# Chunked attention and a gated feed-forward: a planner's choice of engine, order and margin for copies and attention operations

## The chip, the cores and the metric

The kernel runs on one core of a Trainium2 chip. The metric is the device time of one execution in microseconds, the median of several executions. Its engines are called PE (TensorE, matrix products), PEld (TensorE's weight loads), DVE (VectorE), ACT (ScalarE), POOL (GpSimd) and SP (SyncE) in the profile; each works through its own queue in order, and semaphores hold an instruction back until what it needs is done. An instruction that waits holds up all that stand behind it on its engine.

## The reference

Chunked attention with a small memory, and then a gated feed-forward network on its output. Batch 4, 8 heads, 768 positions, 64 numbers a head; 8 memory slots; 3072 tokens, model width 512, inner width 1536; all float32.

```python
for c in range(nc):                          # 24 chunks of 32 positions
    l_start, r_end = max(0, 32*c - 16), min(S, 32*c + 32 + 8)
    k_full = concatenate([mem_k, k[:, :, l_start:r_end]], axis=2)
    v_full = concatenate([mem_v, v[:, :, l_start:r_end]], axis=2)
    scores = scale * matmul(q_c, k_full.transpose(0, 1, 3, 2))
    a = softmax(scores)
    out[:, :, c_start:c_end] = matmul(a, v_full)
x = out.transpose(0, 2, 1, 3).reshape(B * S, H * D)
y = (maximum(x @ w_gate, 0) * (x @ w_val)) @ w_out
```

So each chunk of 32 queries sees 16 positions before it, its own 32, 8 after it and 8 memory slots: 64 slots in all.

## The kernel before, in words

**Tiles.** The 3072 tokens are 24 tiles of 128 (4 chunks each), six tiles a batch. For the feed-forward part they are joined into eight blocks of 2, 2, 2, 4, 4, 4, 4 and 2 tiles (`BLOCKS`), so that block 2 is tiles 4 and 5, block 3 is tiles 6 to 9 and block 4 is tiles 10 to 13.

**Attention of a tile** `a`, each step an operation with a name:
- `t`, `tc`: keys and queries are transposed, by TensorE against an identity (`qk_t`, L275; for batch 0 `pair_t`, L236) into a PSUM slot of the pool `aps`, and copied out by VectorE or ScalarE (`qk_copy`, L79 or L81 of the helper `copy`). From tile 15 on a DMA transposes instead.
- `s`: scores, 32 small products (L309) into the one slot of the pool `sps`.
- `max`, `sub`: VectorE takes the row maximum (L322) and subtracts it (L329); that frees the slot of the scores.
- `exp`: ScalarE, three instructions (L337). `sum`, `rec`, `nrm`: VectorE (L341, L345, L352).
- `p`, `pc`: the probabilities are transposed on TensorE (L358) and copied out; from tile 15 by a DMA.
- `v`, `x`: products with the values (L388; for batch 0 L374 and L381) into a slot of `aps`, copied out into the block's `xT` (L79 or L81).

**Values.** From batch 1 on, v lies in `v_bd` (two sets, used by turns), where each chunk has its 64 slots on partitions: for each half of the heads 32 rows that a DMA brings (`load_v_rows`, L185, operation `vl`), then 24 "upper" rows, which are the first 24 rows of the next chunk, and 8 memory rows (`mem_rows`, L168, `mr`). The upper rows are not loaded but copied within SBUF: `upper` (L190 to L194), 16 copies a batch for batches 1 to 3, 48 in all, 24 rows of 768 or 704 numbers each, operations `up`. In the kernel before they are on VectorE alone. Each waits for the `vl` of its half of the heads, and the values of a tile wait for the copies that they read. The sets must first be zeroed (`zero`, L130 to L136): `z1` for set 1, `z0` for set 0, once batch 0 no longer uses it.

**Feed-forward.** Of a block: for each of 12 inner tiles `m` a gate product and a value product, each four matmuls with as many columns as the block has tokens (L407, operation `f`, PSUM pool `fps` of four banks); relu on ScalarE (L413, `r`); the product of both on VectorE (L419, `g`). Then for each tile of the block the output products, 12 matmuls of 512 columns in four groups of three (L432, `o`), a copy on ScalarE and the store (L437, L439, `oc`). Blocks 0 and 1 are interleaved, by the groups in which the weights are loaded.

**The order of work.** It is set at build time by a planner, `schedule` (L682 to L787), which plays through the whole kernel with written costs and gives every engine a fixed queue. Each operation has the engines that may do it with a cost on each, its dependencies, what must have been started before it (`after`), what slots it takes and gives, and a priority (a tuple, lowest first). Whenever an engine is free in the planner's time, it takes the first operation in the order of priority that is ready: dependencies done, slots free. Feed-forward operations on VectorE and ScalarE have priority 0, attention operations (1, tile, step), feed-forward products on TensorE 2: attention goes ahead of products, and products fill the rest. An attention operation (priority 1) goes to TensorE behind planned 36 us only when its inputs have been done for `MARGIN` in the planner's time (L747, L748); this looks at dependencies, not at slots. A load's landing is estimated from a queue model plus a constant (L740): 1.2 us for the first loads, then 2.4 up to the 45th, and after that 6.0 for `vl` and 4.0 for others. Loads are issued by POOL in a fixed order, and POOL waits on each. What the planner supposes is not what the chip does: if an input is later on the chip than in the plan, the engine waits at that place of its queue.

`pace` (L508) binds the transposes of tiles 6 to 14 to the start of certain feed-forward products, so that attention does not run too far ahead.

Of the kernel before, what the change touches and what calls it, by code (L numbers as in the profile page):

```python
# [14 lines left out]
ACT = mybir.ActivationFunctionType  # L15
# [4 lines left out]
def kernel(  # L20
# [117 lines left out]
    def idle_product(N):  # L138
        if "idle" not in TMP:
            TMP["idle"] = fps.tile([128, 512], F32, tag="fps", name="idle_ps")  # L140
        nc.tensor.matmul(TMP["idle"][:, 0:N], lhsT=idle[:, 0:128], rhs=idle[:, 0:N], start=True, stop=True)  # L141
# [48 lines left out]
    def upper(b, par, i0, i1, eng):  # L190

        x = v_bd[b % NSET].rearrange("p h c d -> p (h c) d")
        d = slice(D * par, D * par + D)
        copy(eng, x[64 * par + CH:64 * par + CTX, i0:i1, d], x[64 * par:64 * par + CTX - CH, i0 + 1:i1 + 1, d])  # L194
# [252 lines left out]
    ops, loads = {}, []  # L447
# [3 lines left out]
    def op(key, eng, fn, deps=(), prio=(0,), take=(), give=(), after=()):  # L451
        ops[key] = dict(eng=eng, fn=fn, deps=list(deps), prio=prio, take=list(take), give=list(give),
                        after=list(after))
# [8 lines left out]
        return {"DVE": (0.07 + 0.52e-3 * n, 0.16 + 0.52e-3 * n), "ACT": psum(n)["ACT"]}  # L462

    engine = {"ACT": nc.scalar, "DVE": nc.vector}
    MARGIN = 0.4


    op("idle", {"DVE": 0.2}, lambda e: nc.vector.memset(idle, 0.0), prio=(-10,))
# [51 lines left out]
    for a in range(NT):  # L520
        b, t = divmod(a, TPB)
# [60 lines left out]
    for rank, (blk, m) in enumerate(seq):  # L582
        n = BLOCKS[blk]
# [34 lines left out]
    for b in range(1, B):  # L618
        for n in range(2 * HP):
            hp, par = divmod(n, 2)  # L620
            for m in range(TPB // UT):
                i0 = NCH * hp + 4 * UT * m
                i1 = min(i0 + 4 * UT, HP * NCH - 1)
                op(("up", b, n, m), {"DVE": 0.1 + 64 * 0.5e-3 * (i1 - i0)},
                   lambda e, b=b, par=par, i0=i0, i1=i1: upper(b, par, i0, i1, engine[e]),
                   [("vl", b, par)], (1, TPB * b - 1 + UT * m, 9), (), (), [("v", TPB * b - 7)] if b > 1 else [])

# [51 lines left out]
    def timed(d):  # L679
        return isinstance(d, tuple) and len(d) == 2 and isinstance(d[1], float)  # L680

    def schedule():  # L682
        done, started, times = {}, set(), [0.7]
        free = {e: 0.7 for e in ("PE", "ACT", "DVE", "SP", "POOL")}
        queue_end, flying, gives = 0.0, [], [(WARM + 0.15, "fps")]
        room["fps"] -= 1
        heapq.heappush(times, WARM + 0.15)
        todo = {e: [] for e in free}
        order, n_load = [], 0
        names = lambda o: [d[0] if timed(d) else d for d in o["deps"]] + o["after"]  # L690
        missing = {k: len(set(names(o))) for k, o in ops.items()}
        users = {}
        for k, o in ops.items():
            for d in set(names(o)):
                users.setdefault(d, []).append(k)

        def offer(k):
            for e in ops[k]["eng"]:
                bisect.insort(todo[e], (ops[k]["prio"], k), key=lambda x: x[0])

        for k in ops:
            if not missing[k]:
                offer(k)

        def ready(o, t, margin=0.0):
            if any(d not in started for d in o["after"]):
                return False
            for d in o["deps"]:
                d, lag = d if timed(d) else (d, 0.0)
                if d not in done or done[d] + lag + margin > t + 1e-9:  # L710
                    return False
            return all(room[r] >= o["take"].count(r) for r in o["take"])

        while len(started) < len(ops) + len(loads):
            t = heapq.heappop(times)
            while times and times[0] <= t + 1e-9:
                heapq.heappop(times)
            for g in [g for g in gives if g[0] <= t + 1e-9]:
                gives.remove(g)
                room[g[1]] += 1  # L720
            flying = [f for f in flying if f > t]
            moved = True
            while moved:
                moved = False
                for e in ("POOL", "PE", "ACT", "DVE", "SP"):
                    if free[e] > t + 1e-9:
                        continue
                    if e == "POOL":
                        if n_load == len(loads):
                            continue  # L730
                        o = loads[n_load]
                        if len(flying) >= 8 or not ready(o, t):
                            continue
                        n_load += 1
                        key = o["key"]
                        if o["n"]:
                            end = t + 0.62 + 0.27e-3 * o["n"]
                            queue_end = max(queue_end, end + 0.8) + o["work"]
                            flying.append(queue_end + 1.0)
                            done[key] = queue_end + (1.2 if n_load < 8 else 2.4 if n_load < 45 else 6.0 if key[0] == "vl" else 4.0)  # L740
                        else:
                            end = done[key] = t + max(o["work"], 0.6)
                        fn = o["fn"]
                    else:
                        o = None
                        for _, key in todo[e]:
                            late_pe = e == "PE" and t > 36.0 and ops[key]["prio"][0] == 1  # L747
                            if ready(ops[key], t, MARGIN if late_pe else 0.0):  # L748
                                o = ops[key]
                                break  # L750
                        if o is None:
                            if e == "PE" and 1.3 < t < WARM:
                                order.append((t, lambda: idle_product(256)))
                                free[e] = t + (0.213 if t < 9.0 else 0.11)
                                heapq.heappush(times, free[e])
                            elif e == "PE" and t <= 1.3:
                                heapq.heappush(times, 1.31)
                            continue
                        for x in o["eng"]:
                            todo[x].remove((o["prio"], key))  # L760
                        d = o["eng"][e]
                        d, lat = d if isinstance(d, tuple) else (d, d)
                        d *= (1.8 if e == "PE" and t < 8.0 and key[0] in ("t", "p", "sh", "f") else 1.0)
                        end = t + d
                        done[key] = end + 0.25 if e == "PE" else t + lat + 0.08

                        if queue_end > t:
                            queue_end += 1.1 if e == "SP" and key[0] in ("t", "pc") else 0.7 if key[0] == "oc" else 0.0
                        fn = lambda o=o, e=e: o["fn"](e)
                        for g in o["give"]:  # L770
                            g, lag = g if isinstance(g, tuple) else (g, 0.0)
                            gives.append((done[key] + lag, g))
                            heapq.heappush(times, done[key] + lag)
                    for r in o["take"]:
                        room[r] -= 1
                    started.add(key)
                    for k in users.get(key, ()):
                        missing[k] -= 1
                        if not missing[k]:
                            offer(k)  # L780
                    order.append((t, fn))
                    free[e] = end
                    for x in (end, done[key], done[key] + 0.2, done[key] + 1.5, done[key] + MARGIN):
                        heapq.heappush(times, x)
                    moved = True
            assert times, [k for k in ops if k not in started][:20]
        return order  # L787

    for _, fn in schedule():
        fn()  # L790
# [30 lines left out]
```

## Time and profile before

| what | value |
|---|---|
| time, median of 3 runs | 246.46 us (245.55 to 247.07) |
| profiled execution, its own time | 246.7 us |
| span from its first to its last instruction | 244.9 us |
| PE busy | 235.3 us, 2706 matmuls |
| DVE busy | 154.0 us |
| ACT busy | 122.0 us |
| POOL busy | 77.7 us |
| copies of v's upper slots on DVE (42 of 768 numbers, 6 of 704) | 15.8 us and 2.6 us |

The profiled execution is one run of its own, 0.24 us over the median; 1.8 us of its time lie outside the span. Rows of the timeline read: start, length, engine, line, operation, what is written from what, number of instructions merged, and in brackets how long the engine stood idle before and what ended it. Rows of the waits read: who waited, for whom, microseconds in total, times, longest. Rows of groups read: line, engine, operation, names, shapes, count, then busy time and mean nanoseconds of one, then idle time before them. TensorE's matmuls are pipelined: the record of one overlaps that of the next.

### The profile page before, as it was taken

Reading aid. Unit: us, or ns where it says so; the run is one execution under the profiler, and the core shown is the slowest. Engines: PE = TensorE matmul, PEld = TensorE weight load, DVE = VectorE, ACT = ScalarE, POOL = GpSimd, SP = SyncE. Lnnn points to the kernel's source line nnn. Section 1 sums busy time; section 2 is a strip of 40 time slices with the busy share of each in tenths; the row PEclk is TensorE's granted clock in tenths of the full one; section 3 lists DMA queues with packets and bytes.
Section 4 is the critical chain, followed back from the end, with each engine's and each line's share of the span. In section 5 each row is a group of like instructions: output and inputs, shape, how many; then the busy total and the mean of one; then the engine's idle time right before and its main releaser. Section 6 shows DMA issues by size and latency. Waiting matters only on the chain.

```text
span 244.9 us, 6549 instructions
## 1 busy us (share of the span) xinstructions
PE 235.3 (96%) x2706; PEld 140.5 (57%) x2706; DVE 154.0 (63%) x313; ACT 122.0 (50%) x271; POOL 77.7 (32%) x102
## 2 busy tenths in 40 slices
PE   7898999999889999899999999999999999999994
PEld 4576887884379644454544544554445444444873
DVE  5664867977979649988648999995432034310430
ACT  7577778693365336755335655354331233312432
POOL 8975679215984099038250000000000000000000
PEclk9999999999999999999999999999999999999999
DMA  6999999999999999999993121443001210002102
GB/s 71 172 178 203 201 163 151 185 130 124 195 180 169 90 139 119 113 159 128 109 226 60 35 42 29 133 122 48 0 0 45 86 43 0 3 35 93 45 0 86
DMA packets 96413, 25.17 MB, mean 103 GB/s; under 512 B 87424, under 2 KB 93312, under 8 KB 96384
## 3 DMA queue, kind: packets, MB, share of 16 engines
q0 software_dynamic: 76128, 14.65, 85.9%
q1 hardware_dynamic: 16656, 3.82, 15.2%
q10 hardware_dynamic: 3600, 6.29, 7.4%
q8 instruction: 21, 0.34, 0.7%
q14 instruction: 8, 0.07, 0.1%
HBM read 28.55 MB, written 6.29 MB: 142 GB/s over the span
## 4 chain that ended last, share of the span: by engine, by line
PE 63%; DMA 18%; DVE 8%; POOL 5%; issue 3%; ACT 2%; ACTq 0%; POOLq 0%; DVEq 0%
PE out_ps L432 21%; PE g_ps L407 19%; PE v_ps L407 18%; DMA v_bd<-in_v_dram 8%; DMA qk_p<-in_q_dram 6%; DMA w_gate_sb<-in_moe_w_gate_dram 4%; DVE v_bd L81 3%; PE xT_ps L388 2%; PE s_ps L309 1%; DVE gvT L419 1%; POOL v_n L199 1%; DVE dif L329 1%; POOL qk_p L227 1%; DVE mx L322 1%; PE pT_ps L358 1%
## 5 line engine op out<-in xcount | busy, mean ns | idle before, releaser
L419 DVE TENSOR_TENSOR gvT<-v_ps,g_relu 128x256 f16<-128x256 f32 (+1 forms) x96 | 52.8, 553 | 55.5 <-PE v_ps L407 40.4
L407 PE MATMUL v_ps<-xT,w_val_sb 128*128 128x256 f16 (+1 forms) x384 | 78.2, 326 | 0.0
L407 PE MATMUL g_ps<-xT,w_gate_sb 128*128 128x256 f16 (+1 forms) x384 | 78.1, 326 | 0.0
L413 ACT ACTIVATE g_relu<-g_ps 128x256 f16<-128x256 f32 (+1 forms) x96 | 46.8, 490 | 50.3 <-PE g_ps L407 49.1
L432 PE MATMUL out_ps<-w_out_sb,gvT 128*128 128x512 f16 (+2 forms) x300 | 66.0, 371 | 0.0
L407 PEld LDWEIGHTS <-w_gate_sb 128*128 128x128 f16 x384 | 36.3, 98 | 23.7
L407 PEld LDWEIGHTS <-w_val_sb 128*128 128x128 f16 x384 | 36.0, 98 | 21.7 <-issue 0.2
L432 PEld LDWEIGHTS <-gvT 128*128 128x128 f16 x300 | 27.9, 98 | 29.5
L79 ACT COPY o_sb<-out_ps 128x512 f32<-128x512 f32 (+2 forms) x25 | 14.2, 568 | 36.6 <-PE out_ps L432 28.5
L337 ACT ACTIVATE p_exp<-dif 128x256 f16<-128x256 f32 (+2 forms) x72 | 19.6, 337 | 11.9 <-DVE dif L329 11.4
L81 DVE COPY v_bd<-v_bd 24x768 f16<-24x768 f16 (+1 forms) x48 | 18.3, 423 | 3.8 <-DMA v_bd<-in_v_dram 3.3
L254 POOL DMA_DIRECT2D qk_b<-in_q_dram x18 | 16.3, 904 | 8.9 <-DMA v_bd<-in_v_dram 5.7
L322 DVE TENSOR_REDUCE mx<-s_ps 128x8 f32<-128x512 f32 x24 | 16.5, 686 | 4.1 <-PE s_ps L309 3.6
L254 POOL DMA_DIRECT2D qk_b<-in_k_dram x18 | 16.3, 904 | 5.4 <-DMA w_out_sb<-in_moe_w_out_dram 4.0
L341 DVE TENSOR_REDUCE sm<-p_exp 128x8 f32<-128x512 f16 x24 | 16.3, 678 | 2.0 <-ACT p_exp L337 1.9
L352 DVE TENSOR_TENSOR p_n<-p_exp,rinv 128x512 f16<-128x512 f16 x24 | 16.5, 686 | 0.3
L329 DVE TENSOR_TENSOR dif<-s_ps,mx 128x512 f32<-128x512 f32 x24 | 16.4, 682 | 0.2
L168 POOL DMA_DIRECT2D v_bd<-vmem x16 | 10.5, 664 | 14.5 <-DMA v_bd<-in_v_dram 13.1
L185 POOL DMA_DIRECT2D v_bd<-in_v_dram x12 | 11.0, 928 | 11.4 <-DVE gvT L419 10.6
L79 ACT CAST xT<-xT_ps 128x512 f16<-128x512 f32 x16 | 9.4, 584 | 8.2 <-PE xT_ps L388 6.5
L388 PEld LDWEIGHTS <-v_bd 128*128 128x128 f16 x288 | 9.8, 96 | 4.0 <-DVE v_bd L81 0.7
L141 PE MATMUL idle_ps<-idle 128*128 128x256 bf16 x69 | 10.7, 302 | 1.1 <-DVE warm L475 1.1
(56 smaller groups left out, 170.7 us busy)
## 6 DMA issues: line engine op xcount, KB each, us to landing
out_dram<-o_sb ACTq DMA_DIRECT2D x23, 256.0 KB
qk_b<-in_k_dram POOLq DMA_DIRECT2D x18, 128.0 KB, 7.5
qk_b<-in_q_dram POOLq DMA_DIRECT2D x18, 128.0 KB, 7.5
v_bd<-in_v_dram POOLq DMA_DIRECT2D x6, 384.0 KB, 12.5
w_out_sb<-in_moe_w_out_dram POOLq DMA_DIRECT2D x2, 768.0 KB, 11.5
qk_p<-in_k_dram POOLq DMA_DIRECT2D x3, 256.0 KB, 5.4
qk_p<-in_q_dram POOLq DMA_DIRECT2D x3, 256.0 KB, 6.8
v_n<-in_v_dram POOLq DMA_DIRECT2D x6, 128.0 KB, 6.5
```

Of the source, the lines that this page charges most:

```text
L79: nc.scalar.copy(o, i)
L81: eng.tensor_copy(o, i)
L254: nc.gpsimd.dma_start(qk_b[a, i], bass.AP(tensor=x.tensor, offset=x[b, 0, 128 * t, 0].offset, ap=[[D, 128], [S * D, H], [1, D]]))
L322: nc.vector.reduce_max(SM[a, "mx"], s4, axis=AX.X)
L329: nc.vector.tensor_tensor(out=SM[a, "dif"].rearrange("p (m r) a s -> p r m a s", r=2), in0=S_ps.pop(a).rearrange("p r (m a) s -> p r m a s ...
L337: nc.scalar.activation(p[:, :, :, s0:s0 + k1 - k0], dif[:, :, :, k0:k1], ACT.Exp, scale=SCALE)
L341: nc.vector.reduce_sum(SM[a, "sm"], SM[a, "p"], axis=AX.X)
L352: nc.vector.tensor_tensor(out=P_n[a], in0=SM.pop((a, "p")), in1=rinv_b, op=ALU.mult)
L407: nc.tensor.matmul(ps, lhsT=w[:, f, 128 * m:128 * m + 128], rhs=xTs[blk][:, f, :], start=(f == 0), stop=(f == NFC - 1))
L413: nc.scalar.activation(st["r", m], st.pop((0, m)), ACT.Relu)
L419: nc.vector.tensor_tensor(out=st["gv"][:, m, :], in0=st.pop((1, m)), in1=st.pop(("r", m)), op=ALU.mult)
L432: nc.tensor.matmul(st["o", t, c], lhsT=st["gv"][:, m, 128 * t:128 * t + 128], rhs=w_out_sb[:, m, c[0]:c[1]], start=(m == 0), stop=(m == ND ...
```

## The change

Four edits, all in the planner and its costs; no computation is changed.

1. The margin of attention operations on TensorE is 1.0 us where it was 0.4. The same constant is among the instants at which the planner looks again (L783).
2. The upper copies may be taken by ScalarE as well, at 0.16 + 64 x 0.0009 us a chunk (0.85 us for 12 chunks); the cost on VectorE is written as 0.52 us for 12 chunks where it was 0.48.
3. The landing of batch 1's v is estimated 4.5 us behind the queue model where it was 2.4.
4. When an engine looks for work, and the first ready operation is an upper copy or a zeroing of set 0, it is not taken if an operation ahead of it in the order of priority is going to be ready within 0.3 us; the engine then stays idle until the planner looks again.

```diff
-    MARGIN = 0.4
+    MARGIN = 1.0
...
-                op(("up", b, n, m), {"DVE": 0.1 + 64 * 0.5e-3 * (i1 - i0)},
+                op(("up", b, n, m), {"ACT": 0.16 + 64 * 0.9e-3 * (i1 - i0), "DVE": 0.1 + 64 * 0.55e-3 * (i1 - i0)},
                    lambda e, b=b, par=par, i0=i0, i1=i1: upper(b, par, i0, i1, engine[e]),
                    [("vl", b, par)], (1, TPB * b - 1 + UT * m, 9), (), (), [("v", TPB * b - 7)] if b > 1 else [])
...
-                            done[key] = queue_end + (1.2 if n_load < 8 else 2.4 if n_load < 45 else 6.0 if key[0] == "vl" else 4.0)
+                            done[key] = queue_end + (1.2 if n_load < 8 else 4.5 if key[:2] == ("vl", 1) else 2.4 if n_load < 45 else 6.0 if key[0] == "vl" else 4.0)
...
                         o = None
+                        soon = False
                         for _, key in todo[e]:
                             late_pe = e == "PE" and t > 36.0 and ops[key]["prio"][0] == 1
                             if ready(ops[key], t, MARGIN if late_pe else 0.0):
-                                o = ops[key]
+                                o = None if soon and key[0] in ("up", "z0") else ops[key]
                                 break
+                            soon = soon or ready(ops[key], t + 0.3)
```

## Prediction

> **What bounds the kernel now.** I read the page's busy table and its slices first, then windows by stage, then TensorE's waits, then the timeline around each of them.
>
> ```profile
> span 244.9 us, 6549 instructions
> ...
> PE 235.3 (96%) x2706; PEld 140.5 (57%) x2706; DVE 154.0 (63%) x313; ACT 122.0 (50%) x271; POOL 77.7 (32%) x102
> ...
> PE   7898999999889999899999999999999999999994
> ...
> PEclk9999999999999999999999999999999999999999
> ```
>
> TensorE is busy for 96% of the span at the full granted clock, so the end moves only where its queue stands still. No part of this change removes or adds a matmul. The windows say where it stands still (first number the length, second PE's busy time, the others PE weight load, DVE, ACT, POOL):
>
> ```profile
> 57.00:75.00 18.00, 16.24 (x235) 10.23 (x234) 14.73 (x31) 8.57 (x21) 13.88 (x17) 1.00 2.58 170
> ...
> 87.00:105.00 18.00, 17.23 (x177) 8.65 (x176) 15.65 (x31) 11.18 (x24) 10.51 (x12) 1.00 1.89 124
> ...
> 125.00:245.00 120.00, 116.81 (x1053) 60.60 (x1050) 59.37 (x109) 46.85 (x102) 0.76 (x1) 1.00 0.22 52
> ```
>
> Two stretches of 18 us hold gaps of 1.76 and 0.77 us. VectorE is at 82% and 87% there, ScalarE at 48% and 62%. After 125 us the 3.2 us that are missing are the tail behind the last matmul, which no edit touches. TensorE's own list of waits names the four gaps:
>
> ```profile
> PE pT_ps L358 <- DVE p_n L352: 1.0, 1, 1.0
> ...
> PE qk_ps L275 <- ACT xT L79: 0.8, 1, 0.8
> ...
> PE xT_ps L388 <- DVE v_bd L81: 0.4, 1, 0.4
> ...
> PE s_ps L309 <- ACT kT L79: 0.3, 1, 0.3
> ```
>
> These idle times are too short, because a matmul's record runs on after the next could have been issued. The chain of waits shows the true rate in an undisturbed stretch, and the timeline shows each gap:
>
> ```profile
> 215.76 10.36 PE out_ps L432 x48
> ```
> ```profile
> 57.75 0.31 PE L309 MATMUL s_ps<-kT,qT 64*32 64x64 bf16 x32
> ...
> 59.95 0.40 PE L388 MATMUL xT_ps<-pT,v_bd 128*128 128x32 f16 x8
> 60.76 0.53 PE L388 MATMUL xT_ps<-pT,v_bd 128*128 128x32 f16 x8 [0.42 <-DVE v_bd L81]
> ...
> 65.16 1.47 PE L432 MATMUL out_ps<-w_out_sb,gvT 128*128 128x512 f16 x6
> 67.67 0.40 PE L358 MATMUL pT_ps<-band,p_n 128*128 128x128 f16 x4 [1.04 <-DVE p_n L352]
> ...
> 69.20 0.56 PE L388 MATMUL xT_ps<-pT,v_bd 128*128 128x32 f16 x16
> ...
> 72.12 0.22 PE L309 MATMUL s_ps<-kT,qT 64*32 64x64 bf16 x6
> 72.64 0.30 PE L309 MATMUL s_ps<-kT,qT 64*32 64x64 bf16 x26 [0.30 <-ACT kT L79]
> ```
> ```profile
> 100.82 1.03 PE L407 MATMUL v_ps<-xT,w_val_sb 128*128 128x512 f16 x4
> 102.62 0.38 PE L275 MATMUL qk_ps<-ident_b,qk_b 128*128 128x128 bf16 x4 [0.78 <-ACT xT L79]
> ```
>
> A product of 512 columns is issued every 10.36/48 = 0.216 us. Gap A, the values of tile 6: 59.95 to 61.29 is 1.34 us, where the undisturbed sixteen take 0.56, so 0.78 lost. Gap B, the transpose of tile 7's probabilities: 65.16 plus 6 x 0.216 is 66.46, it starts at 67.67, 1.21 lost. Gap C, the scores of tile 9: 72.12 to 72.94 is 0.82 against 0.31, 0.51 lost. Gap D, a transpose of keys of tile 13: 100.82 plus 4 x 0.216 is 101.68, it starts at 102.62, 0.94 lost. Together 3.44 us: the most that this change can win behind 36 us, before which the longer margin does not act.
>
> **The change part by part.** *The landing of batch 1's v (4.5 for 2.4) and gaps A and B.* VectorE around them:
>
> ```profile
> 59.40 1.57 DVE L81 COPY v_bd<-v_bd 24x768 f16<-24x768 f16 x4 [1.55 <-DMA v_bd<-in_v_dram]
> 61.00 0.69 DVE L322 TENSOR_REDUCE mx<-s_ps 128x8 f32<-128x512 f32 x1
> 61.72 0.78 DVE L81 COPY v_bd<-v_bd 24x768 f16<-24x768 f16 x1
> 62.54 0.69 DVE L329 TENSOR_TENSOR dif<-s_ps,mx 128x512 f32<-128x512 f32 x1
> ...
> 65.20 0.81 DVE L81 COPY v_bd<-v_bd 24x768 f16<-24x768 f16 x1
> ...
> 66.28 0.61 DVE L81 COPY v_bd<-v_bd 24x768 f16<-24x768 f16 x1
> 66.92 0.69 DVE L352 TENSOR_TENSOR p_n<-p_exp,rinv 128x512 f16<-128x512 f16 x1
> ```
>
> Copies of v's upper slots stand at the head of VectorE's queue and wait 1.55 us for the transfer; tile 7's row maximum stands behind them from 58.06, when its scores end, until 61.00. Then copies of 0.78, 0.81 and 0.61 us stand inside its softmax, 2.20 us in all. The planner supposes the landing 2.1 us too early. With 4.5 it puts those copies and the values of tile 6 2.1 us later, and TensorE runs other output products first, of which this stage has four tiles of twelve. Gap A of 0.78 is under 2.1: it goes. The maximum no longer stands behind the transfer (2.9 us), and a copy is not begun when a softmax operation comes within 0.3 us (up to 2.2 us): 5.1 us against a gap of 1.21: B goes. What is late next is A's wait if ScalarE's copies come late, priced in the rivals.
>
> *The copies shared.* Prices, by form:
>
> ```profile
> L81 DVE COPY v_bd<-v_bd 24x768 f16<-24x768 f16 x42 | 15.8, 420 | 3.7 <-DMA v_bd<-in_v_dram 3.3
> ...
> L134 ACT COPY v_bd<-idle 128x512 f32<-128x512 f32 x7 | 4.0, 617 | 0.0
> ...
> L134 ACT COPY v_bd<-idle 128x1536 f32<-128x1536 f32 x2 | 2.8, 1461 | 0.0
> ```
>
> No upper copy runs on ScalarE now. By its two SBUF copies, (1461 - 617)/1024 = 0.824 ns an element, 768 elements take 617 + 256 x 0.824 = 828 ns, an estimate; the ends are 617 and 1461. Of 48 copies none to all may move, as either engine is free first; I take half: VectorE loses 24 x 0.42 = 10.1 us, ScalarE gains 24 x 0.83 = 19.9 us, spread over three batches. Neither lies on TensorE's path by itself. The Trainium skill, "ScalarE: Activation LUTs", section "Rules for kernel authors", advises VectorE over ScalarE for simple elementwise work, up to about 3x faster per element in bf16. The rows agree in direction (0.42 against 0.83), and by that rule the move is a loss: the first rival. "Perfetto Trace Analysis", section "Optimizing Scalar/DVE Operations", of the same skill says that where VectorE is saturated, giving work to ScalarE may pay; the window at 87% is such a place.
>
> *The margin (1.0 for 0.4).* Behind planned 36 us an attention operation goes to TensorE only 0.6 us later after its inputs. Gap C is 0.51: it goes, if ScalarE is not later than now. Gap D is another kind of wait: the transpose waits for a PSUM slot that tile 10's xT copy frees, and the margin looks at inputs, not at slots. It shrinks only if VectorE, which held up that ScalarE queue, runs earlier; between 0 and 0.94, I take half, 0.47. The price of the margin is latency: four TensorE operations a tile (transpose, scores, probabilities, values), 4 x 0.6 = 2.4 us. Its cover is how long the last xT copy of a block lies ahead of the block's first product:
>
> ```profile
> 81.30 0.59 ACT L79 CAST xT<-xT_ps 128x512 f16<-128x512 f32 x1 [0.44 <-PE xT_ps L388]
> ```
> ```profile
> 87.33 0.86 PE g_ps L407 x4
> ...
> 125.00 0.86 PE g_ps L407 x4
> ```
> ```profile
> 119.20 0.59 ACT L79 CAST xT<-xT_ps 128x512 f16<-128x512 f32 x1 [1.33 <-PE xT_ps L388]
> ```
>
> 87.33 - 81.89 = 5.4 us for block 3, 125.00 - 119.79 = 5.2 for block 4. If the stage ahead of block 3 becomes 2.5 us shorter (A, B, C), 2.9 us are left, still over 2.4. So nothing, by a small surplus.
>
> *DMA queues.* No load changes its place on POOL's queue; batch 2's v load is issued at 68.80, 14.9 us behind the last zeroing that it needs (52.92 + 1.03):
>
> ```profile
> 52.92 1.03 DVE L136 MEMSET v_bd<- 128x512 f32 x2
> ```
> ```profile
> 68.80 1.84 POOL L185 DMA_DIRECT2D v_bd<-in_v_dram  x2
> ```
>
> A zeroing held back by the new rule is covered by that, so nothing.
>
> *New waits.* Another order brings gaps that no row can show. Four of 0.51 to 1.21 stand in the present order behind 36 us; the bounds are none and a full set as now (3.44). I take one of the size of B's and C's mean, (1.21 + 0.51)/2 = 0.86, less than now because margins are longer.
>
> Sum: -0.78 - 1.21 - 0.51 - 0.47 + 0.86 = -2.1 us. The profiled execution took 246.7 us, 0.24 over the median of 246.46, so it would become 244.6 and the median 244.3.
>
> **The rivals.**
> *ScalarE becomes what TensorE waits for.* C and D are already released by ScalarE copies. If one upper copy of 0.83 us stands in front of each of the two, C becomes 1.34 and D 1.77; with A and B gone that is -1.99 + 1.66 = -0.3: 246.1 us. For it: each copy takes twice as long as on VectorE, and the rule against starting one looks only 0.3 us ahead. Against it: ScalarE is idle for 38% and 52% of the two stretches.
> *All gaps go and none come*: 246.46 - 3.44 = 243.0 us. For it: behind 125 us the present order has none. Against: D is not addressed.
> *The attention chain comes too late for block 3* (slower). Latency of margins plus batch 1's later v puts the values of tile 6 up to 2.1 + 0.6 us later, and tiles 7 to 9 behind it; up to 2.7 + 2.4 = 5.1 us on tile 9's xT copy, where 2.9 us are covered. Beyond 2.9 each us is a us. To end over 1% slower it would have to eat the 2.5 us won and 2.5 more, a copy 7.9 us later than now; that takes ScalarE's copies waiting at the head of its queue for the transfer, as VectorE's do now (1.55), with three copies behind them (2.5): 5.1 + 1.55 + 2.5 = 9.2 us late, so 246.46 - 2.5 + 9.2 - 2.9 = 250.3 us. Against it: the transpose of tile 9 is bound to block 2's start and moves ahead with it.
>
> **How the numbers follow.** Forecast 0.45 (its own range 243.4 to 245.4), ScalarE's waits 0.23, all gaps gone 0.19, late chain 0.13. A median of this kernel can be told from no change at about 1%, 2.5 us, so faster is below 244.0 and slower above 248.9. Faster: all of the third (0.19) and 0.19 of the forecast's 0.45, 0.38. Slower: nearly all of the late chain, 0.12. Within 1%: 0.50. The range takes in the three cases without the late chain's worst: 242.8 to 247.6, leaving about 0.17 out.
>
> **What would show it.** Right: in TensorE's waits the rows of values on v_bd, of pT_ps on p_n and of scores on kT are gone; in VectorE's timeline the maximum of tile 7 follows its scores directly; about half of the upper copies stand on ScalarE at 0.8 us; PE is 17.5 us or more of 57:75. Wrong: PE waits on ScalarE's g_relu, kT or xT rows; block 3's first product waits for xT; the copies are much longer than 0.83 us; or the gaps lie where there are none now, behind 105 us.

## The result and the profile after

| | time, median | runs | profiled execution, own time | span |
|---|---|---|---|---|
| before | 246.25 us (245.55 to 247.07) | 6 | 246.7 us | 244.9 us |
| after | 244.76 us (244.19 to 245.30) | 6 | 244.74 us | 242.7 us |

The ratio of after to before is 0.994, with a 95% interval of 0.9917 to 0.9963: 1.5 us faster, small but clear of zero. Medians here take in every run, while ratios leave out single executions that stand far apart from the rest, among them 247.54 us in landing_share, 248.70 us in only_margin (its profiled one) and 1338 us in no_margin. The two profiled executions lie 2.0 us apart, since that of before was 0.45 us above its median.

The page's first part and slices for the changed kernel, and the same three windows as in the prediction (length, then busy time of PE, PE weight load, DVE, ACT, POOL):

```profile
span 242.7 us, 6546 instructions
## 1 busy us (share of the span) xinstructions
PE 235.8 (97%) x2706; PEld 140.8 (58%) x2706; DVE 147.9 (61%) x296; ACT 136.0 (56%) x288; POOL 77.9 (32%) x102
...
PE   7898999999999999999999999999999999999994
```
```profile
57.00:75.00 18.00, 17.75 (x265) 11.94 (x264) 14.50 (x31) 14.99 (x32) 14.61 (x18) 1.00 2.24 185
87.00:105.00 18.00, 18.00 (x210) 8.98 (x208) 15.68 (x32) 15.05 (x31) 7.92 (x9) 1.00 1.93 143
```

In the slices the digits below 9 that PE had near 60 to 75 and 100 us are gone; PE's busy time in the two stretches rose from 16.24 to 17.75 and from 17.23 to 18.00 us. ScalarE went from 48% to 83% and from 62% to 84% in them. VectorE hardly changed there (14.73 to 14.50 and 15.65 to 15.68 us): it does fewer upper copies (7 for 13 and 3 for 9), and other operations stand in their place.

TensorE's own waits in the changed kernel, all that are listed:

```profile
PE idle_ps L141 <- DVE warm L475: 1.1, 1, 1.1
PE qk_ps L236 <- DMA qk_p<-in_q_dram: 0.5, 1, 0.5
PE vs_ps L215 <- DMA v_n<-in_v_dram: 0.5, 1, 0.5
PE qk_ps L236 <- issue: 0.5, 1, 0.5
PE qk_ps L236 <- ACT xT L79: 0.3, 1, 0.3
PE pT_ps L358 <- DVE qT L81: 0.2, 1, 0.2
PE kmem_ps L154 <- DVE ident_f L480: 0.2, 1, 0.2
```

Of the four rows of gaps A to D none is left. All but the sixth row belong to the first 24 us (batch 0's loads and the start). The sixth is new. TensorE's timeline shows it, and two more gaps that have no row among the waits, because the record of the matmul before covers them:

```profile
68.25 0.60 PE L407 MATMUL g_ps<-xT,w_gate_sb 128*128 128x256 f16 x4
69.10 0.38 PE L358 MATMUL pT_ps<-band,p_n 128*128 128x128 f16 x4 [0.25 <-DVE qT L81]
```
```profile
143.50 1.03 PE L407 MATMUL v_ps<-xT,w_val_sb 128*128 128x512 f16 x4
144.66 0.32 PE L309 MATMUL s_ps<-kT,qT 64*32 64x64 bf16 x32
144.91 1.04 PE L407 MATMUL g_ps<-xT,w_gate_sb 128*128 128x512 f16 x4
```
```profile
43.73 0.60 PE L407 MATMUL v_ps<-xT,w_val_sb 128*128 128x256 f16 x4
44.17 0.60 PE L407 MATMUL g_ps<-xT,w_gate_sb 128*128 128x256 f16 x4
44.89 0.60 PE L407 MATMUL v_ps<-xT,w_val_sb 128*128 128x256 f16 x4
```

Four products of 256 columns go out in 0.44 us (43.73 to 44.17) and four of 512 in 0.86. So 69.10 - 68.25 - 0.44 = 0.41 us, 144.66 - 143.50 - 0.86 = 0.30 and 44.89 - 44.17 - 0.44 = 0.28 are lost, 1.0 us together. Each is a wait for a PSUM slot and not for an input. The probabilities of tile 7 had been ready since 67.15; they wait for the slot of `aps` that a copy of queries (VectorE, 68.63 to 69.04) frees. The scores at 144.66 follow the end of the subtraction that frees their only slot (144.51). The value product at 44.89 needs a bank of `fps`, which the relu on ScalarE frees at 44.84.

So the account of the two profiled executions is: four gaps of 3.44 us gone, 1.0 us of new ones, a net of 2.4 us, of which the span shows 2.2; the 0.2 us left over I did not trace.

### The profile page after: what moved, and what is told of

The parts are those of the page before. It is cut to its first block, busy times and chain, and to the rows that moved or that the text cites. A ratio compares the mean times of both kernels' runs of the same rounds, so it can differ in the third digit from the quotient of the medians.

```text
span 242.7 us, 6546 instructions
## 1 busy us (share of the span) xinstructions
PE 235.8 (97%) x2706; PEld 140.8 (58%) x2706; DVE 147.9 (61%) x296; ACT 136.0 (56%) x288; POOL 77.9 (32%) x102
## 4 chain that ended last, share of the span: by engine, by line
PE 88%; ACT 4%; DMA 2%; POOL 2%; DVE 2%; issue 1%; ACTq 0%; POOLq 0%
PE v_ps L407 26%; PE g_ps L407 25%; PE out_ps L432 22%; PE xT_ps L388 3%; DMA v_n<-in_v_dram 2%; PE s_ps L309 2%; PE idle_ps L141 2%; PE vs_ps L215 2%; PE xT_ps L381 2%; PE pT_ps L358 2%; ACT v_bd L79 1%; PE qk_ps L275 1%; PE qk_ps L236 1%; POOL qk_p L227 1%; ACT o_sb L79 1%
## 5 line engine op out<-in xcount | busy, mean ns | idle before, releaser
L432 PE MATMUL out_ps<-w_out_sb,gvT 128*128 128x512 f16 (+2 forms) x300 | 65.3, 371 | 0.0
L337 ACT ACTIVATE p_exp<-dif 128x256 f16<-128x256 f32 (+2 forms) x72 | 19.6, 340 | 4.4 <-DVE dif L329 3.5
L79 ACT COPY v_bd<-v_bd 24x768 f16<-24x768 f16 (+1 forms) x20 | 15.6, 818 | 2.2 <-ACT o_sb L79 1.2
L79 ACT CAST xT<-xT_ps 128x512 f16<-128x512 f32 x17 | 9.9, 583 | 6.2 <-PE xT_ps L388 4.8
L141 PE MATMUL idle_ps<-idle 128*128 128x256 bf16 x69 | 11.5, 319 | 1.1 <-DVE warm L475 1.1
```

The lines of the kernel that those rows point to most:

```text
L79: nc.scalar.copy(o, i)
L337: nc.scalar.activation(p[:, :, :, s0:s0 + k1 - k0], dif[:, :, :, k0:k1], ACT.Exp, scale=SCALE)
L432: nc.tensor.matmul(st["o", t, c], lhsT=st["gv"][:, m, 128 * t:128 * t + 128], rhs=w_out_sb[:, m, c[0]:c[1]], start=(m == 0), stop=(m == ND ...
```

## The experiments

Three theories were open. **Each edit has its gap**: the landing estimate removes A and B, the margin C, the copies shared D. **One edit does it all**, the margin first of all. **It is the order that counts**: any edit makes the planner draw another order, and gaps fall where they fall. In the table, "soon-rule" is the fourth edit, by which a copy or a zeroing is held back when an operation ahead of it will be ready within 0.3 us. "A to D" are the gaps named in the prediction; sizes behind the first 24 us are by the spacing of matmuls, as there. Ratios are to the kernel before, run beside each set on the same chip; its median there was 246.25 us beside after, 245.98 beside the next four rows, 245.62 beside the four from only_margin to only_landing and 245.75 beside the last four, so ratios and not medians compare across the sets.

| kernel | margin | copies shared | landing 4.5 | soon-rule | median us | ratio, 95% interval |
|---|---|---|---|---|---|---|
| after | 1.0 | yes | yes | yes | 244.76 | 0.9940 (0.9917 to 0.9963) |
| no_margin | 0.4 | yes | yes | yes | 246.26 | 1.0008 (0.9983 to 1.0032) |
| no_landing | 1.0 | yes | no | yes | 244.27 | 0.9929 (0.9901 to 0.9958) |
| no_share | 1.0 | no | yes | yes | 244.09 | 0.9926 (0.9901 to 0.9952) |
| nudge | 0.43 | no | no | no | 245.21 | 0.9981 (0.9958 to 1.0004) |
| only_margin | 1.0 | no | no | no | 245.08 | 0.9977 (0.9951 to 1.0003) |
| margin_107 | 1.07 | no | no | no | 245.68 | 1.0004 (0.9972 to 1.0036) |
| after_dve | 1.0 | in the plan, issued on VectorE | yes | yes | 246.34 | 1.0033 (1.0009 to 1.0056) |
| only_landing | 0.4 | no | yes | no | 244.44 | 0.9949 (0.9928 to 0.9970) |
| landing_share | 0.4 | yes | yes | no | 244.20 | 0.9941 (0.9906 to 0.9976) |
| landing_margin | 1.0 | no | yes | no | 244.48 | 0.9940 (0.9914 to 0.9966) |
| after_slot | 1.0, and 0.6 on slots | yes | yes | yes | 244.12 | 0.9920 (0.9890 to 0.9950) |
| landing_slot | 0.4, and 0.6 on slots | no | yes | no | 243.72 | 0.9904 (0.9873 to 0.9934) |

### One edit taken back from the changed kernel

```diff
-    MARGIN = 1.0
+    MARGIN = 0.4
```

> The changed kernel with the margin back at 0.4, the other three edits kept. Theory (each gap has its own edit: the landing estimate removes A and B, the margin C, less load on VectorE D): A and B stay away, waits of the size of C come back, 245.3 to 246.0 us. Rival (the margin does all of it, since it delays the same attention operations as the landing estimate): all gaps come back, 246.2 us. Rival (what counts is only that another order was drawn): anywhere within 1.5 us of 245.5.

Measured: 246.26 us, no faster than before, which looks like the first rival's figure; the second rival's range takes it in too. But its profile does not show the first rival's mechanism: A to D did not come back. One large gap did, at a new place, TensorE waiting for a slot that an xT copy on VectorE frees; and the timelines of ScalarE and VectorE show what stood ahead of that copy:

```profile
68.31 0.60 PE L407 MATMUL v_ps<-xT,w_val_sb 128*128 128x256 f16 x4
69.83 0.38 PE L275 MATMUL qk_ps<-ident_b,qk_b 128*128 128x128 bf16 x4 [0.92 <-DVE xT L81]
```
```profile
66.61 0.83 ACT L79 COPY v_bd<-v_bd 24x768 f16<-24x768 f16 x1 [0.41 <-ACT o_sb L79]
67.45 0.81 ACT L337 ACTIVATE p_exp<-dif 128x256 f16<-128x256 f32 x3
```
```profile
67.04 1.11 DVE L81 COPY v_bd<-v_bd 24x768 f16<-24x768 f16 x1
68.30 0.69 DVE L341 TENSOR_REDUCE sm<-p_exp 128x8 f32<-128x512 f16 x1
69.02 0.20 DVE L345 RECIPROCAL rinv<-sm 128x8 f32<-128x8 f32 x1
69.14 0.64 DVE L81 CAST xT<-xT_ps 128x512 f16<-128x512 f32 x1
```

The exponentials of tile 8 start at 67.45, behind an upper copy on ScalarE that ends at 67.44, though their input was there at 66.68; the row sum waits for them until 68.30, the xT copy stands behind the row sum, and TensorE loses 69.83 - 68.31 - 0.44 = 1.08 us. This looks like the prediction's first rival at work, through VectorE, but ScalarE's copy accounts for little of it. VectorE's own upper copy, of 1.11 us, ends only at 68.15, so without ScalarE's copy the row sum could have begun at most 0.15 us earlier. What delays the xT copy, whose products end at 67.81, is mainly what stands ahead of it on VectorE itself: that upper copy, the row sum and the reciprocal.

Nor does this gap explain the median. The profiled execution took 245.16 us and is one of four runs at 244.82 to 245.16; seven others lie at 246.14 to 246.73, and what these wait for no profile shows.

```diff
-                            done[key] = queue_end + (... else 4.5 if key[:2] == ("vl", 1) else 2.4 if n_load < 45 ...)
+                            done[key] = queue_end + (... else 2.4 if n_load < 45 ...)
```

> The changed kernel with batch 1's landing estimate back at 2.4, the rest kept. Theory: VectorE's and ScalarE's queues again hold copies that wait for the transfer; A (0.78, less the 0.6 of margin) and most of B (1.21) come back, 245.8 to 246.3 us. Rival (the margin alone): 244.8 us, no wait of TensorE on p_n or v_bd.

Measured: 244.27 us. The theory is refuted here: with margin, sharing and soon-rule together, the landing estimate is not needed. Copies at the head of VectorE's and ScalarE's queues do wait for batch 1's transfer again, 1.44 and 0.64 us, but TensorE does not wait for them: no row of its waits names p_n or v_bd, as the rival had it.

```diff
-                op(("up", b, n, m), {"ACT": 0.16 + 64 * 0.9e-3 * (i1 - i0), "DVE": 0.1 + 64 * 0.55e-3 * (i1 - i0)},
+                op(("up", b, n, m), {"DVE": 0.1 + 64 * 0.5e-3 * (i1 - i0)},
```

> The changed kernel with the upper copies on VectorE alone at the old cost, the rest kept. Theory: A, B and C stay away; VectorE is back at 85% or more in the stretch of block 3, and gap D (0.94) comes back, 245.5 to 245.9 us. Rival (sharing does nothing for TensorE): 244.8 us with ScalarE 13 to 16 us less busy. Rival (sharing costs, since a copy takes 0.82 instead of 0.42 us): below 244.5 us.

Measured: 244.09 us. VectorE alone does the copies and D does not come back:

```profile
57.00:75.00 18.00, 17.91 (x269) 12.40 (x267) 15.63 (x35) 10.76 (x25) 13.77 (x16) 1.00 2.41 177
87.00:105.00 18.00, 18.00 (x209) 9.05 (x207) 16.42 (x35) 10.23 (x22) 10.09 (x12) 1.00 1.97 138
```

VectorE stands at 91% in the second window, more than before the change (87%), and TensorE has no idle time in it. So a VectorE as busy as that does not by itself make gap D. The time is where the second rival put it, but whether sharing costs, the two intervals overlap too far to say.

### How much is the order alone?

```diff
-    MARGIN = 0.4
+    MARGIN = 0.43
```

> The kernel before with the margin at 0.43 instead of 0.40 and nothing else: a change too small to mean anything, which only makes the planner draw a slightly different order. Theory: gaps A and B are there as before, 246.0 to 246.5 us. Rival (any other order moves the time): over 0.7 us away from 246.25, with gaps at other places.

Measured: 245.21 us, an interval that just holds 1. In its profile A and C are gone, and B and D are there as before: by spacing 1.36 us before a pT_ps that waits for p_n, and 0.98 us before a qk_ps that waits for xT. So two of the four gaps (1.29 us) vanished in the profile of an edit that means nothing, and a time that moves by half a microsecond proves nothing about an edit.

```diff
-    MARGIN = 0.4
+    MARGIN = 1.0
```

> The kernel before with the margin at 1.0 and nothing else. New theory (the margin does it, the other three edits are not needed for the gain): gaps A to D are gone or under 0.3 us each, 244.0 to 244.8 us. Rival (margin and soon-rule together, which are the two edits that all good kernels so far share): B comes back, since copies stand inside tile 7's softmax, 245.2 to 246.0 us.

Measured: 245.08 us, not told apart from before. Neither theory's figure; the margin by itself does not give the gain. Which gaps its usual execution has is not shown.

```diff
-    MARGIN = 0.4
+    MARGIN = 1.07
```

> The kernel before with the margin at 1.07 and nothing else: another order from nearly the same rule. Theory (the margin does it whatever order comes out): within 0.5 us of the kernel with 1.0, gaps behind 36 us below 1.0 us in all. Rival (the good order at 1.0 was a lucky draw): 245 to 246.3 us with a gap of about 1 us at a new place.

Measured: 245.68 us, ratio 1.0004: the margin alone gives no time. Its profile, at 245.72 us close to the median, is not quite the rival's either. None of A to D is in it, though VectorE's copies wait 1.92 us for the transfer and tile 7's maximum stands behind them until 62.52:

```profile
59.37 3.11 DVE L81 COPY v_bd<-v_bd 24x768 f16<-24x768 f16 x7 [1.92 <-DMA v_bd<-in_v_dram]
62.52 0.69 DVE L322 TENSOR_REDUCE mx<-s_ps 128x8 f32<-128x512 f32 x1
```

The largest gap left is a slot wait of 0.60 us, 69.82 - 68.78 - 0.44, with others of 0.2 to 0.4 us. So a profile without the four gaps does not yet mean a shorter median. The prediction took their sizes from an execution of 246.7 us, and the median of before beside this set is 245.62 us: a usual execution of before probably loses less in gaps than 3.44 us, by an estimate from these two times about 1 us less.

### Moving the copies with the order held

```diff
-                   lambda e, b=b, par=par, i0=i0, i1=i1: upper(b, par, i0, i1, engine[e]),
+                   lambda e, b=b, par=par, i0=i0, i1=i1: upper(b, par, i0, i1, nc.vector),
```

> The changed kernel with its order and all its queues' sequence kept, but the 20 upper copies that it gives to ScalarE issued on VectorE at the same places of the order. Theory (sharing itself is off TensorE's path): 244.3 to 245.0 us, ScalarE about 15 us less busy and VectorE about 8 us more. Rival (VectorE needs the relief): TensorE waits on VectorE in the stretch of block 3, 245.3 to 246.5 us.

Measured: 246.34 us; the rival, though not in the stretch of block 3 mainly (0.54 us are lost there, before a pT_ps that waits for p_n). TensorE, in the timeline, loses 1.76 us at the place where the changed kernel loses 0.41:

```profile
68.23 0.60 PE L407 MATMUL g_ps<-xT,w_gate_sb 128*128 128x256 f16 x4
70.43 0.38 PE L358 MATMUL pT_ps<-band,p_n 128*128 128x128 f16 x4 [1.60 <-DVE qT L81]
```

Held to an order that was planned for two engines, one engine is late. With an order planned for one engine (no_share) it is not. I take it that what counts is that order and duration agree, not which engine does the copies; these two runs are all that show it.

### The landing estimate, alone and with others

```diff
-                            done[key] = queue_end + (... else 2.4 if n_load < 45 ...)
+                            done[key] = queue_end + (... else 4.5 if key[:2] == ("vl", 1) else 2.4 if n_load < 45 ...)
```

> The kernel before with the landing of batch 1's v at 4.5 instead of 2.4 and nothing else. The prediction's step: A and B go (2.0 us), C and D stay: 244.0 to 244.5 us. Rival (the copies leave the wait for the transfer, but the margin of 0.4 leaves other operations as close as before): A goes, B or others of its size come, 245.5 to 246.3 us.

Measured: 244.44 us, ratio 0.9949: alone it brings nearly all that the four edits bring together. VectorE's timeline shows the step as the prediction had it:

```profile
56.43 1.16 DVE L81 COPY v_bd<-v_bd 24x768 f16<-24x768 f16 x4
57.66 0.69 DVE L322 TENSOR_REDUCE mx<-s_ps 128x8 f32<-128x512 f32 x1
58.38 0.35 DVE L81 COPY v_bd<-v_bd 24x768 f16<-24x768 f16 x1
58.76 0.69 DVE L329 TENSOR_TENSOR dif<-s_ps,mx 128x512 f32<-128x512 f32 x1
59.48 1.90 DVE L81 COPY v_bd<-v_bd 24x768 f16<-24x768 f16 x4
...
63.19 0.69 DVE L352 TENSOR_TENSOR p_n<-p_exp,rinv 128x512 f16<-128x512 f16 x1
```

Tile 7's maximum now stands ahead of the copies that wait for the transfer (57.66; before 61.00), and its probabilities are done at 63.88 instead of 67.61. Was the transfer only earlier in this execution? The view of the tile v_bd gives the longest time from issue to landing, before first and then this kernel:

```profile
DMA to landing us min/median/max: 4.1/10.2/19.3
```
```profile
DMA to landing us min/median/max: 3.1/9.7/19.6
```

Hardly: 19.6 against 19.3 us from an issue 0.5 us earlier, so it landed at 59.1 us where it had been 59.4, and A, B and C are gone all the same. The planner's own times, played through from the source, agree with the step: the plan of before has this load landed at 57.0 us, 2.4 us before the trace does, and issued at 39.0, where the trace has 40.1; with 4.5 the plan has it landed at 59.1 us.

The twelve runs lie between 243.95 and 244.78 us, the 35 of before beside them between 244.09 and 248.85. What is left in the profile is a slot wait of D's kind, 99.89 - 98.53 - 0.86 = 0.50 us:

```profile
98.53 1.03 PE L407 MATMUL v_ps<-xT,w_val_sb 128*128 128x512 f16 x4
99.89 0.38 PE L275 MATMUL qk_ps<-ident_b,qk_b 128*128 128x128 bf16 x4 [0.34 <-ACT xT L79]
```

With the landing estimate kept, one more edit each, as in the diffs above:

> The kernel before with the landing estimate 4.5 and the upper copies shared with ScalarE, margin 0.4, no soon-rule. Theory (a copy of 0.83 us on ScalarE stands in front of exponentials, and at a margin of 0.4 TensorE feels it): the gain of the landing estimate alone is lost, 245.3 to 246.5 us, a gap behind ScalarE's copies between 60 and 75 us. Rival (what was lost without the margin came from the soon-rule or from the order drawn): 244.1 to 244.8 us, as with the landing estimate alone.

Measured: 244.20 us, so the theory falls: sharing does not undo the gain, and what no_margin lost came from the soon-rule or the order that came out with it. Its single runs spread up to 247.54 us, which I cannot explain; the landing estimate alone does not make the runs even.

> The kernel before with the landing estimate 4.5 and the margin 1.0, copies on VectorE alone, no soon-rule. Theory (the landing estimate carries the gain, the margin adds at most the rest of C): 243.9 to 244.6 us. Rival (the margin hurts where nothing needs it): over 244.9 us.

Measured: 244.48 us, the same as the landing estimate alone. In its profile the largest gap left is a slot wait of 0.58 us (a transpose of keys at 106.66, behind an xT copy).

### A margin on slots

What the profiles of the faster kernels had left behind 24 us was mainly waits for slots, to which the margin is blind (no_share and only_landing each have also a transpose that waits for loaded keys, 0.25 and 0.18 us). So the planner was told that a slot of `aps` comes free 0.6 us after its copy:

```diff
+    SLOT = 0.6
...
-                (1, a - i, 0), (), ["aps"])
+                (1, a - i, 0), (), [("aps", SLOT)])
...
-            op(("pc", a), psum16(HP * 128), lambda e, a=a: p_copy(a, engine[e]), [("p", a)], (1, a, 9), ["pT"], ["aps"])
+            op(("pc", a), psum16(HP * 128), lambda e, a=a: p_copy(a, engine[e]), [("p", a)], (1, a, 9), ["pT"], [("aps", SLOT if b else 0.0)])
...
-        op(("x", a), psum(HP * 128), lambda e, a=a: x_copy(a, engine[e]), [("v", a)], (1, a, 11), (), ["aps"],
+        op(("x", a), psum(HP * 128), lambda e, a=a: x_copy(a, engine[e]), [("v", a)], (1, a, 11), (), [("aps", SLOT if b else 0.0)],
```

> The changed kernel with a margin on slots too: the planner takes a slot of the pool aps for free only 0.6 us after its copy has ended, from batch 1 on. Theory (the gaps that are left are waits for slots, at which the margin does not look): the wait of pT_ps on the qT copy (0.41 us by spacing) goes and nothing of its kind comes, 244.0 to 244.6 us. Rival (two slots are too few to hold each longer): attention falls behind, 245 us or more, with TensorE waiting for an xT copy at the start of a block.

Measured: 244.12 us. The wait of 0.41 us is gone; the two of 0.3 us for other pools (near 44 and 144 us) stayed, as they should.

> The kernel before with the landing estimate 4.5 and the 0.6 us on slots, margin 0.4, copies on VectorE alone, no soon-rule. Theory: its gap of 0.50 us (a transpose of keys that waits for the slot of an xT copy near 99 us) goes, 243.7 to 244.3 us, the fastest of all. Rival: the same as the landing estimate alone, 244.4 us, with a slot gap at another place.

Measured: 243.72 us, ratio 0.9904 (0.9873 to 0.9934), the lowest of all. Its windows and all rows of its waits on TensorE:

```profile
57.00:75.00 18.00, 18.00 (x266) 12.41 (x265) 16.26 (x35) 11.63 (x29) 14.83 (x18) 1.00 2.21 184
87.00:105.00 18.00, 18.00 (x224) 9.32 (x223) 17.14 (x36) 10.34 (x23) 8.76 (x11) 1.00 2.05 144
```
```profile
PE qk_ps L236 <- issue: 1.2, 1, 1.2
PE idle_ps L141 <- DVE warm L475: 1.1, 1, 1.1
PE qk_ps L236 <- DMA qk_p<-in_q_dram: 0.5, 1, 0.5
PE kmem_ps L154 <- DMA kmem_f<-in_mem_k_dram: 0.4, 1, 0.4
PE qk_ps L236 <- ACT xT L79: 0.3, 1, 0.3
PE vs_ps L215 <- DMA v_n<-in_v_dram: 0.3, 1, 0.3
PE qk_ps L236 <- DMA qk_p<-in_k_dram: 0.2, 1, 0.2
```

All of these lie in the first 24 us. Behind them, by the spacing of starts, no gap of over 0.13 us is left on TensorE, with VectorE at 95% in the second window. The time is at the lower end of the theory's range. Its interval overlaps that of the changed kernel (0.9917 to 0.9963), so the two are not told apart; it has two small edits instead of four. The margin on slots was never run by itself.

## Why the prediction was right, and where it was not

*The bound.* Right: only TensorE's gaps could be won. They were 3.44 us in the profile of before, and landing_slot's profile has none of them and no new one. How much of them a usual execution of before loses is not shown; its profile ran 0.45 us over the median beside it, and up to 1.1 us over the later ones.

*Landing estimate, A and B gone.* That the estimate is enough was right: only_landing shows it with an equally long transfer, and A and B are in none of the nine profiles that have it. That it is needed, as the theory for no_landing had it, was wrong: A is also gone under a mere nudge, and both are gone in margin_107 and, with the other three edits, in no_landing. So in the changed kernel itself the estimate is redundant.

*Copies shared.* The duration was right (828 ns estimated; the group row of the changed kernel follows), and 20 of 48 moved, where 24 were supposed. ScalarE's busy time rose by 14.0 us, VectorE's fell by 6.1 (19.9 and 10.1 were supposed).

```profile
L79 ACT COPY v_bd<-v_bd 24x768 f16<-24x768 f16 x17 | 13.4, 827 | 1.8 <-ACT o_sb L79 0.8 <-DMA qk_b<-in_q_dram 0.4 <-DMA v_bd<-vmem 0.4
```

The failed step is gap D: "It shrinks only if VectorE, which held up that ScalarE queue, runs earlier". D went with VectorE busier than before (no_share, 91%). What removed it is not isolated: it is there in nudge, a wait of its kind is half as long in only_landing (0.50 us), and each of these kernels has another order. The rule from the Trainium skill ("ScalarE: Activation LUTs", "Rules for kernel authors") that I weighed is borne out as far as it goes: 0.827 us against 0.436 on VectorE in the changed kernel, and no loss could be measured from leaving the copies there. The other ("Perfetto Trace Analysis", "Optimizing Scalar/DVE Operations"), that relief may pay where VectorE is saturated, is not borne out here: a VectorE busy for 91 or 95% of a stretch cost TensorE nothing in it.

*The margin, C gone.* C went, but it did not need the margin: C is gone at 0.43 as well, and in only_landing at 0.4, and the margin alone gives 0.9977 and 1.0004. The step that the margin does not look at slots was right, and it was the more useful one.

*New gaps.* Estimated 0.86 us from the size of the old ones, measured 1.0. I had D half left (0.47), and it went whole. So the gaps by themselves come to -2.4 us where the sum says -2.1; the spans differ by 2.2, the profiled times by 2.0, and the medians moved by 1.5, to 244.76 where 244.3 was forecast. That the number came out so near is partly luck: two of the four terms, C by the margin and D by a relieved VectorE, are not shown to have gone for the reasons given, and the gaps were read from a longer execution of before than a usual one.

*The rivals.* The late chain did not come: block 3's last xT copy ends at 80.4 and its first product starts at 85.7, 5.3 us against 5.4 before. That a copy of v on ScalarE holds TensorE up is shown in no run; the nearest is no_margin, where it explains at most 0.15 of 1.08 us. (The idle shares of ScalarE given there belong the other way round, 52% to the first stretch and 38% to the second; nothing hangs on it.) That all gaps go is landing_slot, at 243.72 us, where the rival had 243.0.

*What stays open.* Why margin, sharing and soon-rule do without the landing estimate while sharing, soon-rule and landing estimate without the margin give nothing. The edits do not add up; each draws a new order, and I have one profile of each. Sharing alone, the soon-rule alone and the margin on slots alone were not run, so what each does by itself is not shown.

## What to carry to other kernels

In a kernel whose queues are fixed by a planner, look for the place where the plan is wrong about the chip (here one transfer that landed 2.4 us after its planned time) and mend that number before adding margins or moving work. Take the sizes of gaps from an execution near the median, or compare several: one profile of a longer run promises too much. A margin has to cover every kind of wait, slots as well as inputs. And nudge the planner once with an edit that means nothing: if that alone removes some of the gaps, an ablation by single edits cannot tell causes apart without the trace.

## What the runs showed of the hardware

The same transfer of v, issued at 39 to 40 us behind the same loads, landed 17.8 us (landing_margin and no_margin) to 19.9 us (after_slot and margin_107) after its issue, with 18.1 in the changed kernel and 19.3 before; in only_margin's execution of 248.7 us it took 21.5. Each is one profile of another kernel, so how much of these differences comes from the kernel's order and how much from the single execution is not separated. A plan made for one profile's landing can be wrong by about 2 us in the next.

An upper copy on VectorE took between 335 and 840 ns in the kernel before, and 1.11 us in no_margin while POOL issued a transfer of v; on ScalarE it took 768 to 832 ns in every kernel that gives it some. The rows of the changed kernel:

```profile
L81 DVE COPY v_bd<-v_bd x28: 336/347/776, 56.2 to 121.7; 24x768 f16<-24x768 f16 x25, 24x704 f16<-24x704 f16 x3
L79 ACT COPY v_bd<-v_bd x20: 771/826/832, 55.5 to 122.1; 24x768 f16<-24x768 f16 x17, 24x704 f16<-24x704 f16 x3
```

What lengthens a copy on VectorE goes with POOL's work: in the kernel before the 21 copies that overlap no POOL instruction took 335 to 354 ns, and all of over 0.5 us are among the 27 that do overlap one, at 335 to 840. The Trainium skill, "SBUF — State Buffer", section "Terms", says that VectorE and GpSimd share a pair of SBUF ports under a lock while ScalarE has its own. The rows fit that; no run here separated it from other causes.
